# A new order for the opening of a gated-linear-attention and feed-forward kernel

## The chip, the cores and the metric

The kernel runs on one core of a Trainium2 chip. The metric is the device time of one execution in microseconds (us). A core has TensorE (PE in the profile; its weight loads are a row of their own, PEld), VectorE (DVE), ScalarE (ACT), GpSimd (POOL) and SyncE (SP). Each engine works through its own list of instructions in order and waits at an instruction until the semaphores that it names are reached. SP issues the DMAs here.

## The reference

Attention with a decaying state, per batch and head, and then a feed-forward layer with a squared ReLU:

```python
for t in range(S):
    state = alpha[:, :, t, :, None] * state + np.einsum('bhd,bhe->bhde', k[:, :, t], v[:, :, t])
    y[:, :, t] = np.einsum('bhd,bhde->bhe', q[:, :, t], state)
# x: y as (B*S, H*D)
h = np.maximum(x @ w_in, 0.0)
return (h * h @ w_out).astype(np.float32)
```

There are 4 batches, 8 heads, 768 positions and a head dimension of 48; x is 3072 x 384, w_in 384 x 2048 and w_out 2048 x 384. All is float32.

## The kernel before

The sequence is cut into blocks of 128 positions of one batch, with all eight heads: 24 blocks. Block n is chunk n // 4 of batch n % 4. Four blocks make a group of 512 rows of x, on which the feed-forward layer works: 16 products of 128 hidden columns (layer in), then the products with w_out (layer out). While TensorE works on the feed-forward layer of one group, the attention steps of the next blocks are woven in at planned times. Only the first four blocks (0 to 3) have nothing to be woven into. Their steps, together with the first loads, the first weight conversions and the first products of layer in, stand in a list of words written out by hand, `AT["first"]`; a loop near the end of the kernel runs the words in order, and each engine gets its instructions in that order. This list is the opening.

Before the list come the fixed preparations. POOL clears the state tiles s, the eight pads of the q and k tiles (16 unused columns beside each head's 48) and further tiles, and builds the identity and the triangle of ones (causal, rounded into causal_r; halves_mask is cut from it). VectorE clears two tiles am. `AT["pre"]` names the first loads, and three matmuls on a cleared tile (warm) follow.

The words of one block n, in the order of their data, with the lines of the kernel before:

- load: alpha (a), q, k, v of the block, one DMA each (L109). Some blocks use lent tiles (a_lent, qk_lent).
- ln (L261, ScalarE): logarithm of alpha. cs (L283, TensorE): its prefix sums, a product with the triangle, two passes of 384 columns. eb and ei (L294, L298, ScalarE): exponentials of the sums and of their negatives, called b and inv.
- mq, mk (L302, VectorE): q times b and k times inv, in place. qT, kT (L354, TensorE): turned by products with the identity, 128 x 512 in PSUM. qc, kc (L368): copied into SBUF as qs and ks.
- sc (L413, TensorE): the scores, 32 small products into two PSUM banks. kv (L442, TensorE): the sums of k times v into the same banks. am (L424, VectorE): the masked scores copied out. us (L456, VectorE): the first half's sum plus the old state. lt (L337 on TensorE, copied on ScalarE at L344): the last row of b turned. st (L477, L479, VectorE): the next state.
- For the pairs (0, 1) and (2, 3): ya and yb (L393, TensorE): the outputs y in two PSUM tiles, in two passes with a handshake through POOL between them. ep (L616): x rows copied out of y, 12 copies a pair, in four parts ep0 to ep3. The copies of the even and odd heads overlap in some rows, so that one waits for the other.

Weights come as raw halves of words: weights (L109) loads the next piece, first (L179, ScalarE) and second (L192 to L199, VectorE) convert it. Piece i serves products 2i and 2i + 1. ha and hb (L919) are a product of layer in on the first pair's rows and on the second pair's; ScalarE applies relu (L925) and square (L928). zeros n (L381) is n matmuls on a cleared tile, whose result nobody reads; so is warm (L237).

A copy of qc and kc goes to VectorE where the block's name stands in `AT["cp"]`:

```python
copy = nc.vector.tensor_copy if f"{x}{n}" in AT["cp"] else nc.scalar.copy
```

In the kernel before the names there end in a or b (q2a, k0b), so none matches and ScalarE makes all eight. `AT["evd"]` names the x copies of ep, as (block, even or odd heads, part), that VectorE makes; the others are ScalarE's.

Loads are paced by `move` (L109): an issue on SP waits for the earlier DMA that lies at least 2.25 us back by the costs given to each, 1.1 for a block's tensor and 2.3 for a piece of weights. Among tensors alone this is the fourth-last; behind a piece of weights it is the one ahead of the piece. So an issue marks the landing of an earlier load.

Of the kernel before, what the change touches and what calls it, by code (L numbers as in the profile page):

```python
# [9 lines left out]
FP32 = mybir.dt.float32  # L10
FP32R = mybir.dt.float32r
# [7 lines left out]


GB = 4
AT = {'thrp': 4.5, 'cvo': 3.35, 'thr': 2.25, 'm48': 16, 'cvs': 3.9, 'cv1': 0.125, 'later': (0, 0, 4, 6, 0, 1, 0), 'evs': 0.1, 'lead': 4, 'post': 3, 'w_first': (46.0, 38.0, 49.0), 'wstep': 1.0, 'w_in_at': 2.5, 'w_in_by': 3.6, 'room1': 22, 'room': 24, 's0': 4, 'ahead': 6, 'late': 2, 'xs': 0.0, 'g0': ((0.5, 4, False, True, 27.75), (25.75, 6, True, True), (29.25, 8, True, False)), 'sc0': (3.25, 2.35, 2.35), 'g1': ((5.5, 8, False, 15.0), (13.0, 10, True), (35.25, 12, True)), 'g': ((2.075, 6, True), (14.25, 8, True)), 'g1x': 51.0, 'gx': 48.75, 'g0x': 56.25, 'k0': 2, 'h0': 15, 'k1': 4, 'h1': 3, 'h1by': 2, 'evs0': 0.7, 'tp': 'ADMD', 'tp1': 'ADAD', 'split': 8, 'o0': (46.5, 48.5), 'o1': (), 'o2': (21.25, 24.75, 24.5, 40.0, 35.25, 28.25), 'str1': 21.5, 'ga': 9.75, 'gb': 12.5, 'cv0': -1.25, 'pre': '1a 0a 0q 0k 1k 1q', 'cp': ('q2a', 'k2b', 'k0a', 'k3a', 'k3b', 'k0b', 'q0b', 'q3b', 'q2b', 'q3a'), 'evd': ((0, 0, 0), (0, 0, 1), (0, 1, 2), (0, 1, 3), (2, 0, 3), (2, 1, 1), (2, 1, 2)), 'first': 'ln0 load1v cs0 ei0 eb0 zeros4 mk0 mq0 qT0 kT0 ln1 cs1 kc0 ei1 warm0 load0v eb1 mk1 qc0 weights0 lt1 sc0 load2a mq1 load2q kT1 kc1 qT1 load2k load3a qc1 load3k kv0 am0 first0 load3v sc1 ln2 kv1 load3q us0 am1 weights6 us1 cs2 ya0 ei2 second0 eb2 lt0 ln3 yb0 load2v mq2 qT2 mk2 load4a ep00 ep01 qc2 kT2 cs3 kc2 eb3 ei3 zeros1 sc2 ep02 mq3 mk3 kT3 ep03 weights2 first1 st0 ha0 second1 lt2 kv2 am2 qT3 load4k kc3 qc3 ha1 weights5 first2 sc3 kv3 am3 load4q us2 ha2 us3 ya2 yb2 weights3 ep20 ep21 ep22 load4v ep23 second2 first3 weights1 st1 weights4 ha3 lt3 hb0 st2 second3 hb2 hb3 hb1 st3'}


RUN = {0: 128, 32: 32, 64: 64, 96: 32}
# [3 lines left out]
def kernel(  # L29
# [12 lines left out]
    nc = tc.nc  # L42
    B, H, S, D = q.shape
    C = 128
# [19 lines left out]
    def kept(name, n, shape):  # L64
        return [consts.tile(shape, FP32, name=f"{name}{i}") for i in range(n)]

    s_all = kept("s", B + 2, [128, NP, 64])
    u_all = kept("us", 3, [128, NP, 64])
    for t in s_all[0:B]:
        nc.gpsimd.memset(t, 0.0)  # L70
    s_t = [s_all.pop(0) for _ in range(B)]
    NV = 4
    tiles = {
        "a": kept("a_in", 2, [128, H * D]), "q": kept("q_in", 2, [128, H, 64]),
        "k": kept("k_in", 3, [128, H, 64]), "v": kept("v_in", NV, [128, H * D]),
    }
    for t in tiles["q"] + tiles["k"]:
        nc.gpsimd.memset(t[:, :, D:64], 0.0)

    NW = 8  # L80
    wt_pool = ctx.enter_context(tc.tile_pool(name="wt", bufs=26))
# [2 lines left out]
    def two_k(name, dt=FP32, shape=(GB * C,)):  # L84
        return two_pool.tile([128, *shape], dt, tag="two", name=name)
# [40 lines left out]
    def need(*keys):  # L126
        for key in keys:
            assert key in given, key

    def load(n, xs="aqkv"):  # L130
        c, b = divmod(n, B)
        for x in xs:
            t = tile_of(x, n)
            if id(t) in owner:
                need(("free", *owner[id(t)]))
            owner[id(t)] = x, n
            given.add((x, n))
# [62 lines left out]

    for word in AT["pre"].split():
        load(int(word[0]), word[1:])
# [12 lines left out]
    ident = consts.tile([128, 128], FP32, name="ident")  # L215
    make_identity(nc, ident)
    causal = cv_pool.tile([128, C], FP32, tag="upper", name="causal")
    make_upper_triangular(nc, causal, 1.0, diag=True)
    causal_r = consts.tile([128, C], FP32R, name="causal_r")
    nc.gpsimd.tensor_copy(out=causal_r, in_=causal)  # L220
    halves_mask = consts.tile([128, C // 2], FP32, name="halves_mask")
    for i in range(2):
        rows = slice(64 * i, 64 * (i + 1))
        nc.gpsimd.tensor_copy(out=halves_mask[rows], in_=causal[rows, rows])
    for t in s_all + u_all:
        nc.gpsimd.memset(t, 0.0)
    last = consts.tile([128, 4, NP], FP32, name="last")
    nc.gpsimd.memset(last, 0.0)
# [7 lines left out]
    def warm(_):  # L236
        nc.tensor.matmul(  # L237
            out=ps_att.tile([128, NP, 64], FP32, tag="att", name="warm"),
            lhsT=s_t[0].rearrange("a p d -> a (p d)")[:, 0:128], rhs=s_t[0], start=True, stop=True,
        )  # L240

    for _ in range(3):
        warm(0)
# [11 lines left out]
    def work(name, bufs=1):  # L255
        return p2.tile([128, NP, C], FP32, tag=name, name=name, bufs=bufs)
# [7 lines left out]

    SPLIT = AT["split"]

# [162 lines left out]
    def am_h(n):  # L429
        t = am_t[n // 2 % NAM].rearrange("a e p t -> a (e p t)")  # L430
        return t.rearrange("a (e m p t) -> a e m p t", e=2, m=2, p=NP)

    def state_sums(n):
        need(("v", n), ("kb", n))
        given.add(("free", "k", n))
        ps = two[n]
        m = D if n >= AT["m48"] else 64
        for p in range(NP):
            for e in range(2):
                first = (2 * p + e) * D  # L440
                for h in range(1 if n // B == NCH - 1 else 2):
                    nc.tensor.matmul(  # L442
                        out=ps[h][64 * e : 64 * e + m, 1, p, G:64],
                        lhsT=tile_of("k", n)[HALF[h], 2 * p + e, 0:m],
                        rhs=tiles["v"][n % NV][HALF[h], first : first + D],
                        start=True, stop=True, skip_group_check=True,
# [17 lines left out]
    def rows_of(n):  # L464
        return [slice(0, D), slice(64, 64 + D)] if n >= AT["m48"] else [slice(0, 128)]

# [174 lines left out]
    here, todo, room = {}, [], [22]  # L641
# [92 lines left out]
    def in_x(j):  # L734
        acc["h", j] = ps_ffn.tile([128, GB * C], FP32, tag="att", name="h")
        in_passes(j, "b", "a", True, False)
        in_passes(j, "l", "l", False, True)
        x = acc["h", j]
        if kinds[0][j % 4] == "D":
            hid[j] = two_k("hid")  # L740
            nc.scalar.activation(out=hid[j], in_=x, func=AF.Copy, scale=E)  # L741
        else:
            nc.scalar.activation(out=x, in_=x, func=AF.Copy, scale=1.0 + E)  # L743

    def in_y(j):
        given.add(("hy", j))
        in_passes(j, "d", "d", False, True)
        if kinds[0][j % 4] == "D":
            combine(((hid[j], acc.pop(("h", j)), ALU.add, hid[j]),))

    kinds = [""]

    def in_post(j):
        need(("hy", j))
        given.add(("h", j))
        if kinds[0][j % 4] == "D":
# [7 lines left out]
        if kinds[0][j % 4] == "M":  # L764
# [212 lines left out]
    first = AT["first"]  # L977
# [129 lines left out]
    cv0 = AT["cv0"]  # L1107
    cvs = AT["cvs"]
# [70 lines left out]
```

## Time and profile before

| What | Value |
|---|---|
| Median of three runs | 518.93 us (517.73 to 519.45) |
| Profiled execution: span from first to last instruction | 518.6 us |
| Profiled execution: its own time beside the span | not listed; 0.3 us lie between the span and the median of the runs |
| TensorE busy | 507.8 us (98%) |
| VectorE, ScalarE, POOL busy | 355.7, 306.4, 5.3 us |
| TensorE busy from 0.00 to 5.67 us | 2.93 us, all of it on cleared tiles |
| TensorE busy from 15 to 25 us | 7.54 of 10 us |
| VectorE and ScalarE busy from 15 to 25 us | 9.50 and 7.77 of 10 us |
| TensorE busy from 25 to 37 us | 11.70 of 12 us |
| DMA engines' busy share from 15 to 37 us | 0.92 to 0.94 |

Times within the profile count from the first instruction. A row of a timeline gives start, length, engine, line, operation, output and inputs, and in brackets how long the engine had been idle and which instruction released it; x4 means four instructions drawn together. Lengths of neighbouring instructions overlap by about 0.1 us on VectorE and ScalarE, and by more on TensorE, so a chain is added up from start to start.

### The profile page before, as it was taken

How to read it: one execution, taken by the hardware profiler on the slowest of the kernel's cores; microseconds unless marked ns; L12 is line 12 of the kernel's file. 1: busy time of each engine (PE TensorE's matmuls, PEld its weight loads, DVE VectorE, ACT ScalarE, POOL GpSimd, SP SyncE). 2: the span in 40 equal slices, each digit the busy share in tenths (PEclk: the TensorE clock that was granted, in tenths of full speed). 3: DMA queues.
4: the chain of work that ended last, by engine and by line, in shares of the span. 5: the costliest groups of instructions: out<-in, count | busy, mean ns of one | idle time of the engine just before them, and what ended most of it. 6: DMA issues, size and time to landing. Idle time of an engine off the chain costs nothing.

```text
span 518.6 us, 13019 instructions
## 1 busy us (share of the span) xinstructions
PE 507.8 (98%) x5338; PEld 418.9 (81%) x5338; DVE 355.7 (69%) x628; ACT 306.4 (59%) x649; POOL 5.3 (1%) x29
## 2 busy tenths in 40 slices
PE   7899999999999999999999999999999999999997
PEld 5675455678888669987899988899988899988997
DVE  2766669986887877776697468587465487363861
ACT  4788898547888653485664276772275673164620
POOL 4000000000000000000000000000000000000000
PEclk9999999999999999999999999999999999999999
DMA  9999779472777786898884688864683545699201
GB/s 183 204 267 237 197 189 235 93 228 80 238 190 184 246 243 162 265 279 227 205 225 143 222 247 222 223 200 152 213 274 124 185 121 154 207 380 322 65 2 61
DMA packets 139323, 102.34 MB, mean 197 GB/s; under 512 B 109808, under 2 KB 115968, under 8 KB 139264
## 3 DMA queue, kind: packets, MB, share of 16 engines
q1 hardware_dynamic: 139264, 101.51, 68.2%
q8 instruction: 42, 0.69, 0.6%
q14 instruction: 17, 0.14, 0.1%
HBM read 84.16 MB, written 17.33 MB: 196 GB/s over the span
## 4 chain that ended last, share of the span: by engine, by line
PE 93%; DVE 4%; issue 1%; POOL 1%; ACT 1%; DVEq 0%; POOLq 0%
PE o L809 39%; PE h L726 32%; PE h L919 8%; PE y L393 4%; PE sckv L413 2%; PE T L578 2%; PE sckv L442 2%; PE cs L283 1%; PE cs L286 1%; DVE x L616 1%; PE cs L287 1%; DVE hd L648 1%; DVE hx L653 0%; DVE am L424 0%; ACT x L616 0%
## 5 line engine op out<-in xcount | busy, mean ns | idle before, releaser
L726 PE MATMUL h<-xd,wd 128*128 128x512 f32 x240 | 68.1, 396 | 1.1 <-issue 1.1
L726 PE MATMUL h<-xa,wb 128*128 128x512 f32 x240 | 68.7, 394 | 0.0
L726 PE MATMUL h<-xl,wl 128*128 128x512 f32 x240 | 67.9, 391 | 0.0
L648 DVE TENSOR_TENSOR hid<-h,hid 128x512 f32<-128x512 f32 x40 | 27.6, 689 | 51.1 <-PE h L726 51.0
L616 ACT COPY x<-y 48x256 f32<-48x256 f32 (+3 forms) x133 | 46.7, 365 | 21.2 <-PE y L393 18.8
L809 PE MATMUL o<-wb,ha 128*128 128x384 f32 x160 | 54.5, 340 | 0.0
L743 ACT ACTIVATE h<-h 128x512 f32<-128x512 f32 x40 | 23.3, 582 | 52.3 <-PE h L726 52.3
L809 PE MATMUL o<-wl,hl 128*128 128x384 f32 x160 | 53.7, 336 | 0.1
L809 PE MATMUL o<-wd,hd 128*128 128x384 f32 x304 | 53.7, 334 | 0.0
L809 PE MATMUL o<-w_out,hid 128*128 128x384 f32 x160 | 53.6, 489 | 0.0
L726 PEld LDWEIGHTS h<-xl,wl 128*128 128x128 f32 x240 | 45.1, 188 | 10.1 <-DVE xl L653 0.4
L809 PEld LDWEIGHTS o<-wd,hd 128*128 128x128 f32 x304 | 52.8, 188 | 0.0
L726 PEld LDWEIGHTS h<-xa,wb 128*128 128x128 f32 x240 | 44.4, 188 | 9.8 <-ACT hid L763 0.4
L726 PEld LDWEIGHTS h<-xd,wd 128*128 128x128 f32 x240 | 44.0, 188 | 9.1
L809 PE MATMUL o<-wb,hx 128*128 128x384 f32 x144 | 48.3, 336 | 0.0
L809 PE MATMUL o<-wl,hx 128*128 128x384 f32 x144 | 48.1, 334 | 0.0
L809 PEld LDWEIGHTS o<-w_out,hid 128*128 128x128 f32 x160 | 30.0, 190 | 19.7
L741 ACT ACTIVATE hid<-h 128x512 f32<-128x512 f32 x40 | 24.2, 606 | 32.9 <-PE h L726 32.5
L919 PE MATMUL h<-x,w_in 128*128 128x512 f32 (+1 forms) x120 | 43.4, 512 | 0.2 <-DVE x L616 0.2
L701 ACT ACTIVATE ha<-hid 128x512 fp32r<-128x512 f32 x40 | 25.1, 642 | 20.3 <-PE o L809 7.9
L919 PEld LDWEIGHTS h<-x,w_in 128*128 128x128 f32 x120 | 22.1, 190 | 17.8 <-issue 15.3
L653 DVE SCALAR_TENSOR_TENSOR hl<-ha,hid 128x512 fp32r<-128x512 f32 x40 | 27.5, 687 | 6.9 <-ACT ha L701 6.8
(111 smaller groups left out, 852.5 us busy)
## 6 DMA issues: line engine op xcount, KB each, us to landing
wd<-do SPq DMA_DIRECT2D x36, 384.0 KB
wl<-lo SPq DMA_DIRECT2D x34, 384.0 KB
wl<-li SPq DMA_DIRECT2D x32, 384.0 KB
wd<-di SPq DMA_DIRECT2D x32, 384.0 KB
raw<-in_moe_w_out_dram SPq DMA_DIRECT2D x8, 767.5 KB
raw<-in_moe_w_in_dram SPq DMA_DIRECT2D x8, 767.2 KB
v_in<-in_v_dram SPq DMA_DIRECT2D x24, 192.0 KB
out_dram<-osb SPq DMA_DIRECT2D x24, 192.0 KB
```

The costliest lines, as they stand in the source:

```text
L393: ins = nc.tensor.matmul(out=ys[e][64 * half : 64 * half + D + G * e, m % 2, p // 2, t], lhsT=lhsT, rhs=rhs, start=(half, e) not in seen, ...
L413: nc.tensor.matmul(out=ps[e][HALF[h], 0, p, :], lhsT=ks[rows, p, HALF[h]], rhs=qs[rows, p, HALF[h]], start=True, stop=True, skip_group_che ...
L442: nc.tensor.matmul(out=ps[h][64 * e : 64 * e + m, 1, p, G:64], lhsT=tile_of("k", n)[HALF[h], 2 * p + e, 0:m], rhs=tiles["v"][n % NV][HALF[ ...
L616: copy(out=x[kk][to : to + m, t : t + 2], in_=blk[n]["y"][e][r : r + m, :, p // 2],)
L648: nc.vector.tensor_tensor(out=o, in0=x, in1=z, op=op)
L653: nc.vector.scalar_tensor_tensor(out=o, in0=x, scalar=c, in1=y, op0=ALU.mult, op1=op)
L701: nc.scalar.activation(out=a, in_=x, func=AF.Copy, scale=NEAR * E)
L726: nc.tensor.matmul(out=acc["h", j], lhsT=here[w, "i", p][:, kk, jj * 128 : (jj + 1) * 128], rhs=x_parts[x][:, kk], start=start and kk == 0 ...
L741: nc.scalar.activation(out=hid[j], in_=x, func=AF.Copy, scale=E)
L743: nc.scalar.activation(out=x, in_=x, func=AF.Copy, scale=1.0 + E)
L809: nc.tensor.matmul(out=acc[t][:, 0:DM], lhsT=lhs[:, t * C : (t + 1) * C], rhs=rhs, start=start, stop=stop, skip_group_check=True,)
L919: nc.tensor.matmul(out=ps, lhsT=w[:, kk, c0 : c0 + 128], rhs=xT[g][kk][:, cols], start=(kk == 0), stop=(kk == KM - 1),)
```

## The change

Only the preparations and the opening's tables change.

- On POOL one state tile (s3) is cleared first, then the triangle, its rounded copy and the identity are made, and then the other clears follow. warm reads s3 instead of s0. The eight pads are cleared by VectorE, ahead of its two am tiles.
- `pre` loads k of block 1 ahead of k of block 0.
- `cp` becomes k0, k1, k2, q0, q1: these five turned tiles are copied by VectorE; q2, k3 and q3 stay with ScalarE.
- `evd`: for both pairs VectorE makes the copies of one of the two y tiles (six), ScalarE those of the other (six). Before, it was six and six in the first pair, five and seven in the second.
- `first` is a new list. ln1 and cs1 follow ln0 and cs0 directly; the first weights are loaded ahead of v1; zeros stand in five places (four of one matmul, one of four) where before there were zeros4 and zeros1; st0 stands ahead of the last x copies of the first pair; qT3 ahead of kT3; lt3 ahead of kv2; k3, v2 and v3 are loaded behind the second weights; hb1 is the first product on the second pair; ha4 and hb4 are added, so product 4 is made in halves here instead of whole behind the opening. first0 stands ahead of ln2 in both.
- `j % 4` becomes `j % len(kinds[0])`; the strings have four letters.

```diff
-'pre': '1a 0a 0q 0k 1k 1q', 'cp': ('q2a', 'k2b', 'k0a', 'k3a', 'k3b', 'k0b', 'q0b', 'q3b', 'q2b', 'q3a'), 'evd': ((0, 0, 0), (0, 0, 1), (0, 1, 2), (0, 1, 3), (2, 0, 3), (2, 1, 1), (2, 1, 2)), 'first': 'ln0 load1v cs0 ei0 eb0 zeros4 mk0 mq0 qT0 kT0 ln1 cs1 kc0 ei1 warm0 load0v eb1 mk1 qc0 weights0 lt1 sc0 load2a mq1 load2q kT1 kc1 qT1 load2k load3a qc1 load3k kv0 am0 first0 load3v sc1 ln2 kv1 load3q us0 am1 weights6 us1 cs2 ya0 ei2 second0 eb2 lt0 ln3 yb0 load2v mq2 qT2 mk2 load4a ep00 ep01 qc2 kT2 cs3 kc2 eb3 ei3 zeros1 sc2 ep02 mq3 mk3 kT3 ep03 weights2 first1 st0 ha0 second1 lt2 kv2 am2 qT3 load4k kc3 qc3 ha1 weights5 first2 sc3 kv3 am3 load4q us2 ha2 us3 ya2 yb2 weights3 ep20 ep21 ep22 load4v ep23 second2 first3 weights1 st1 weights4 ha3 lt3 hb0 st2 second3 hb2 hb3 hb1 st3'
+'pre': '1a 0a 0q 1k 0k 1q', 'cp': ('k0', 'k1', 'k2', 'q0', 'q1'), 'evd': ((0, 0, 0), (0, 0, 1), (0, 0, 2), (0, 0, 3), (2, 0, 0), (2, 0, 1), (2, 0, 2), (2, 0, 3)), 'first': 'ln0 ln1 load0v weights1 cs0 load1v cs1 eb0 mq0 ei0 warm0 qT0 zeros1 mk0 qc0 zeros1 kT0 load2a eb1 zeros4 ei1 mk1 kc0 zeros1 kT1 sc0 mq1 kc1 qT1 load2q load2k zeros1 qc1 kv0 am0 first0 load3a load3q lt1 sc1 kv1 ln2 lt0 us0 cs2 am1 eb2 us1 second0 ei2 ya0 weights6 load3k mq2 ln3 mk2 yb0 load2v load3v ep00 cs3 eb3 qT2 ep01 kT2 mq3 weights5 qc2 weights3 kc2 ei3 st0 ep02 qT3 sc2 ep03 mk3 am2 first1 ha0 kT3 weights4 kc3 qc3 ha1 lt3 first2 kv2 sc3 load4k second1 us2 kv3 am3 ha2 us3 ya2 lt2 yb2 st1 load4v ep20 ep21 ep22 ep23 weights0 st3 ha3 load4a hb1 first3 second2 load4q second3 hb0 st2 hb2 hb3 hb4 ha4 weights2'
...
-    for t in s_all[0:B]:
-        nc.gpsimd.memset(t, 0.0)
     s_t = [s_all.pop(0) for _ in range(B)]
+    nc.gpsimd.memset(s_t[3], 0.0)
+    causal = cv_pool.tile([128, C], FP32, tag="upper", name="causal")
+    make_upper_triangular(nc, causal, 1.0, diag=True)
+    causal_r = consts.tile([128, C], FP32R, name="causal_r")
+    nc.gpsimd.tensor_copy(out=causal_r, in_=causal)
+    ident = consts.tile([128, 128], FP32, name="ident")
+    make_identity(nc, ident)
...
-    for t in tiles["q"] + tiles["k"]:
-        nc.gpsimd.memset(t[:, :, D:64], 0.0)
+    pads = tiles["q"] + tiles["k"]
...
-        nc.gpsimd.memset(t[:, :, D:64], 0.0)
+        pads.append(t)
...
+    for t in pads:
+        nc.vector.memset(t[:, :, D:64], 0.0)
...
-    for t in s_all + u_all:
+    for t in s_t[0:3] + u_all + s_all:
         nc.gpsimd.memset(t, 0.0)
...
-            lhsT=s_t[0].rearrange("a p d -> a (p d)")[:, 0:128], rhs=s_t[0], start=True, stop=True,
+            lhsT=s_t[3].rearrange("a p d -> a (p d)")[:, 0:128], rhs=s_t[3], start=True, stop=True,
```

In the words weights0 to weights6 the figure has no effect: each loads the next piece, so both lists load pieces 0 to 6 in order.

More of the change, by code (lines that the diff above doesn't have):

```diff
@@ new lines @@
+AT = {'thrp': 4.5, 'cvo': 3.35, 'thr': 2.25, 'm48': 16, 'cvs': 3.9, 'cv1': 0.125, 'later': (0, 0, 4, 6, 0, 1, 0), 'evs': 0.1, 'lead': 4, 'post': 3, 'w_first': (46.0, 38.0, 49.0), 'wstep': 1.0, 'w_in_at': 2.5, 'w_in_by': 3.6, 'room1': 22, 'room': 24, 's0': 4, 'ahead': 6, 'late': 2, 'xs': 0.0, 'g0': ((0.5, 4, False, True, 27.75), (25.75, 6, True, True), (29.25, 8, True, False)), 'sc0': (3.25, 2.35, 2.35), 'g1': ((5.5, 8, False, 15.0), (13.0, 10, True), (35.25, 12, True)), 'g': ((2.075, 6, True), (14.25, 8, True)), 'g1x': 51.0, 'gx': 48.75, 'g0x': 56.25, 'k0': 2, 'h0': 15, 'k1': 4, 'h1': 3, 'h1by': 2, 'evs0': 0.7, 'tp': 'ADMD', 'tp1': 'ADAD', 'split': 8, 'o0': (46.5, 48.5), 'o1': (), 'o2': (21.25, 24.75, 24.5, 40.0, 35.25, 28.25), 'str1': 21.5, 'ga': 9.75, 'gb': 12.5, 'cv0': -1.25, 'pre': '1a 0a 0q 1k 0k 1q', 'cp': ('k0', 'k1', 'k2', 'q0', 'q1'), 'evd': ((0, 0, 0), (0, 0, 1), (0, 0, 2), (0, 0, 3), (2, 0, 0), (2, 0, 1), (2, 0, 2), (2, 0, 3)), 'first': 'ln0 ln1 load0v weights1 cs0 load1v cs1 eb0 mq0 ei0 warm0 qT0 zeros1 mk0 qc0 zeros1 kT0 load2a eb1 zeros4 ei1 mk1 kc0 zeros1 kT1 sc0 mq1 kc1 qT1 load2q load2k zeros1 qc1 kv0 am0 first0 load3a load3q lt1 sc1 kv1 ln2 lt0 us0 cs2 am1 eb2 us1 second0 ei2 ya0 weights6 load3k mq2 ln3 mk2 yb0 load2v load3v ep00 cs3 eb3 qT2 ep01 kT2 mq3 weights5 qc2 weights3 kc2 ei3 st0 ep02 qT3 sc2 ep03 mk3 am2 first1 ha0 kT3 weights4 kc3 qc3 ha1 lt3 first2 kv2 sc3 load4k second1 us2 kv3 am3 ha2 us3 ya2 lt2 yb2 st1 load4v ep20 ep21 ep22 ep23 weights0 st3 ha3 load4a hb1 first3 second2 load4q second3 hb0 st2 hb2 hb3 hb4 ha4 weights2'}
@@ L214 @@
     nc.scalar.preload_act_table_set("natural_log_exp_and_others")
[L215 to L220, printed above, removed]
     halves_mask = consts.tile([128, C // 2], FP32, name="halves_mask")
@@ L738, in in_x @@
         x = acc["h", j]
-        if kinds[0][j % 4] == "D":
+        if kinds[0][j % len(kinds[0])] == "D":
             hid[j] = two_k("hid")
@@ L747, in in_y @@
         in_passes(j, "d", "d", False, True)
-        if kinds[0][j % 4] == "D":
+        if kinds[0][j % len(kinds[0])] == "D":
             combine(((hid[j], acc.pop(("h", j)), ALU.add, hid[j]),))
@@ L755, in in_post @@
         given.add(("h", j))
-        if kinds[0][j % 4] == "D":
+        if kinds[0][j % len(kinds[0])] == "D":
             h = hid[j]
@@ L763, in in_post @@
         nc.scalar.activation(out=h, in_=acc.pop(("h", j)), func=AF.Relu)
-        if kinds[0][j % 4] == "M":
+        if kinds[0][j % len(kinds[0])] == "M":
             combine(((h, h, ALU.mult, h),))
```

1 line of the change is left out of this document (removed).

## The prediction, made before the changed kernel ran

> **What bounds the kernel now.** I read the page's busy shares first, then its 40 slices, then the opening instruction by instruction: TensorE's timeline, VectorE's, ScalarE's, and the DMA issues on SP.
>
> ```profile
> PE 507.8 (98%) x5338; PEld 418.9 (81%) x5338; DVE 355.7 (69%) x628; ACT 306.4 (59%) x649; POOL 5.3 (1%) x29
> ...
> PE   7899999999999999999999999999999999999997
> ```
>
> TensorE is the bound of nearly the whole span; only the first two slices (26 us) are short of nine tenths. The change rearranges just this stretch, so the most it can win is what TensorE loses there.
>
> ```profile
> 1.10 2.93 PE L237 MATMUL warm<-s 128*128 128x256 f32 x6 [1.10 <-POOL s L70]
> 5.67 1.62 PE L283 MATMUL cs<-a_in,causal_r 128*128 128x384 f32 x2 [1.64 <-POOL us L226]
> 7.08 1.92 PE L381 MATMUL zeros<-s 128*128 128x128 f32 x8
> 8.93 1.11 PE L354 MATMUL qT<-ident,q_in 128*128 128x128 f32 x4
> 10.35 0.81 PE L283 MATMUL cs<-a_in,causal_r 128*128 128x384 f32 x2
> ...
> 17.25 0.91 PE L283 MATMUL cs<-a_lent,causal_r 128*128 128x384 f32 x2 [1.06 <-ACT a_lent L261]
> ...
> 24.35 0.63 PE L354 MATMUL kT<-ident,qk_lent 128*128 128x128 f32 x4 [0.86 <-DVE qk_lent L302]
> 24.82 1.46 PE L919 MATMUL h<-x,w_in 128*128 128x256 f32 x6
> ...
> 35.60 1.23 PE L919 MATMUL h<-x,w_in 128*128 128x256 f32 x4
> 37.04 9.73 PE L919 MATMUL h<-x,w_in 128*128 128x256 f32 x32 [0.21 <-DVE x L616]
> ```
>
> The columns are start, length, instruction and, in brackets, idle time and its releaser. Useful work starts at 5.67 and is unbroken from 37.04 on. Between lie waits (1.06, 0.86), fillers (zeros, warm) and a slow stretch: prefix sums (cs) took 1.62 at 5.67 and 0.81 at 10.35. I compare both kernels at one point, the end of the first half product of the second pair of blocks (hb0 before, hb1 after): 37.04 + 0.43 = 37.47 before. All before it is equal work in both kernels; behind it TensorE has no wait for 200 us.
>
> ```profile
> 16.24 0.78 DVE L424 COPY_PREDICATED am<-halves_mask,sckv 128x256 f32<-128x256 uint32 x2 [0.19 <-PE sckv L442]
> ...
> 19.15 0.96 DVE L199 TENSOR_TENSOR w_in<-w_in,power 128x768 f32<-128x768 f32 x1
> 20.03 0.55 DVE L302 TENSOR_TENSOR qk_lent<-qk_lent,b 128x384 f32<-128x384 f32 x1
> ...
> 21.05 2.22 DVE L616 COPY x<-y 48x256 f32<-48x256 f32 x5
> ...
> 24.24 0.42 DVE L616 COPY x<-y 64x256 f32<-64x256 f32 x1
> ```
>
> From 16.24 to 24.66 VectorE never rests, and its last x copy releases ha0 at 24.82. That chain of 8.42 us, not TensorE, sets the middle of the opening.
>
> ```profile
> 5.04 0.52 ACT L261 ACTIVATE a_in<-a_in 128x384 f32<-128x384 f32 x1 [3.03 <-DMA a_in<-in_alpha_dram]
> ...
> 14.88 1.91 ACT L179 ACTIVATE power<-raw,rebias 128x768 uint16<-128x768 int16 x2
> 16.67 0.53 ACT L261 ACTIVATE a_lent<-a_lent 128x384 f32<-128x384 f32 x1
> ...
> 30.25 1.89 ACT L179 ACTIVATE power<-raw,rebias 128x768 uint16<-128x768 int16 x2
> ```
>
> Here the reader sees three DMA-bound starts: the first logarithm as alpha 0 lands, the conversion of weights 0 at 14.88, that of weights 2 at 30.25.
>
> **The triangle ahead of the clears.** The first cs (5.67) follows the logarithm that ends at 5.04 + 0.52 = 5.56. The triangle's cast was at 4.00 + 0.29 on POOL, 1.3 us ahead; making it sooner gains 0. The bracket's "POOL us" is a clear that happened to end then. The eight pad clears go to VectorE: the 1024-wide clear takes 0.91, a POOL pad clear 0.20, so 8 x 0.1 to 0.9 = 0.8 to 7.2; nearest in width is POOL's row, so about 1.6, ending near 4.7. VectorE's first real work is at 7.84, so 0; only the upper end would make it wait. POOL's remaining clears (it was done at 6.19) serve steps from 14.5 on: 0.
>
> **Prefix sums, fillers, first turns.** cs1 follows cs0 directly (7.08 to 8.36 slow) in place of the 1.71 us of zeros, then warm0 (slow, 0.85) to 9.21, then qT0, ready since 8.45. cs1, which ran at 10.35 to 11.0, is thus done early, but qT0 is 0.28 later. k0 is now loaded behind k1. SP's fourth-last rule makes the weight load wait for the fifth load: issued at 8.56, so k0 lands about 8.55, its product ends at 9.15, ahead of kT0 (10.5 after two one-matmul zeros). zeros4 and another (1.1 us) follow, so kT1 starts near 12.0 (13.22 before).
>
> **Copies on two engines.** No row shows VectorE copying 128x512 out of PSUM. On ScalarE it is 0.585. Bounds: VectorE's 256-wide x copy, 0.42, and two of them, 0.84; nearest is its 512-wide sum from PSUM (hid, 0.689), so 0.69, and 0.60 start to start, as its other rows overlap by 0.1. Queue on VectorE: qc0 10.25, mk1, kc0 to 12.0, mq1, kc1 (12.7, waits for kT1), qc1 13.8 to 14.5, am0 at 14.55 (15.04 before). Behind: lt1 0.46, sc1 0.52, kv1 0.58, and am1 at 16.1 (16.24 before). With 0.42 or 0.84 a copy, am1 moves by some 0.3 either way.
>
> **Loads.** Weights 0 go ahead of v1, which lands 0.6 to 1.1 us sooner, near 14.0 (14.66 before, where a3's issue waited for it). So its conversion ends near 16.0, ln2 at 16.7 and cs2 runs from 16.75: 0.5 earlier. But VectorE converts only behind us1 (16.9), so this early cs2 is cover, not gain. k3, v2 and v3 move behind weights 1; they are needed at 25.4, 28.5 and 29.4 and, at the 0.6 to 1.4 us between their landings and 3.1 for weights, are due by about 25. On SP the later issues wait only for DMAs and for buffers released by conversions.
>
> **VectorE's chain.** From am1 to the last x copy it gains kc2 (0.60) and the state step st0 (0.82, from 24.69 to 25.51 behind ha0's copies before) and loses mk3 (0.47): 8.42 + 0.95 = 9.37, so from 16.1 it ends at 25.47, 0.8 later than before. While it runs TensorE waits, mostly for mq3 (21.3 to 22.6). But qT3 and two thirds of ha0 run beneath its end, so only the last third of ha0 (0.43) follows: ha0 ends at 25.95, 0.26 sooner than before (24.82 + 1.39 = 26.21).
>
> **From ha0 to the second pair.** Before, 26.21 to 33.65 is 7.44. After: 0.46 more for lt3, 0.13 until mk3, 0.1 less as lt2 covers the POOL handshake between the two passes of y (32.95 to 33.02): 7.93, ending at 33.88. Then x: ScalarE starts 0.12 later, VectorE 0.39 behind it (a pair of copies overlaps in rows, 33.77 to 34.16), with six copies at 0.45 (six and six, where it was seven and five; the first pair had six and six already): 3.2, then 0.43 for the last third: 37.5. Before, this took 33.65 to 37.47 with lt3 (0.46) in it.
>
> Sum: 37.5 against 37.47, equal. With am1 at 15.8 and unhindered x copies (0.43, no handover) it is 0.7 earlier. I take the middle, 0.3 earlier. ha4 and hb4 replace one whole product, 6 x 0.43 either way: 0. `% len(kinds[0])` is 4 as before: 0. The profiled span is 518.6; only the span is given for that execution, 0.3 under the 518.93 median. Span 518.6 - 0.3, plus 0.3 to the median: 518.6.
>
> [...] The 128-column passes took 0.21 through 9.8 and 0.11 from 10.0, though the granted clock is 1.00 throughout; TensorE had then been busy 4.3 us. I keep the switch near 9.9: both kernels are busy from 5.67 without a gap. [...]
>
> **Rivals.** (a) *Slow clock for longer.* If cs1, warm0 and the turns do not wake the array by 10 and it stays slow till the scores, then qT0's rest, kT0, kT1, sc0 (some 1.5 us) double; VectorE's copies follow, and am1 comes 1.5 later: 520.1. For it: qT ran slow to 9.8. Against: before, the same mixture woke it. 0.06.
>
> (b) *Slower: ScalarE stuck at weights 2.* Its conversion first2 stands in order before ha2's relu, lt2's copies and the x copies at 34.0: 1.9 + 0.8 + 0.33, so weights 2 must land by 30.9; each us later costs one. They landed at 30.2 before, and the conversion waited for them (30.25). After, alpha 4 is no longer ahead (-0.7), but the issue waits for weights 1. From 33 on this decides for slower: 518.6 + 2.1 = 520.7 or more. With dearer copies (0.84, six on the path: +0.9) it takes less. 0.18.
>
> (c) *Faster: TensorE fed throughout.* If VectorE's chain did not hold ha0 (copies at 0.42, x copies well overlapped), TensorE goes from cs3 (19.85) through qT2, kT2, qT3, sc2, ha0 at 0.5, 0.5, 0.5, 0.6, 1.4 to 23.9 with its waits for mq2: 2 us sooner, 516.5. For it: the order offers work ahead of ha0. Against: 9.4 us of VectorE's rows cannot shrink by 2. A share of it (1.6) is enough. 0.22.
>
> **How the numbers follow.** A measurement here tells about 0.3% (1.6 us) from no change. Equal: 0.54, and rival (a), 0.06, falls inside that bound: same 0.60. Faster 0.22 from (c), slower 0.18 from (b). The range reaches into both: 516.7 (near (c)'s end) to 520.5 (near (b)'s).
>
> **What would show it.** cs0 still at 5.6 to 5.7; cs1 directly behind; the first VectorE copy of qT near 10.3 and 0.6 to 0.7 long; am1 near 16; VectorE without rest to 25.5; a TensorE wait of about 1.3 for mq3; ha0's last third near 25.5; weights 2's conversion by 30; TensorE unbroken from about 37. Wrong if ScalarE waits long for weights 2, if a bank wait appears that the rows cannot show, or if TensorE has waits behind 37.

## The result, and the profile after

The changed kernel took 524.14 us (median of 4 runs, 523.48 to 524.69) against 519.11 us for the kernel before on the same chip (4 runs, 517.73 to 519.45): a ratio of 1.0102, 95% interval 1.0086 to 1.0117. The forecast was no change, 518.6 us with a range up to 520.5. It was wrong: the kernel is 1.0% slower.

The page of the changed kernel, its busy shares, two rows of its 40 slices and one of its DMA queues (packets, MB, share of 16 engines):

```profile
PE 510.2 (98%) x5350; PEld 421.5 (81%) x5350; DVE 360.5 (69%) x642; ACT 304.5 (58%) x645; POOL 4.2 (1%) x21
PE   8899999999999999998999999999999999999997
PEclk9999999999999999998999999999999999999999
q8 instruction: 42, 0.69, 0.5%
```

TensorE has 12 matmuls and 12 weight loads more than before. Of the first two slices, which the change is about, the first is a little fuller (8 tenths in place of 7). New is a dent in the 19th slice (235 to 248 us), in TensorE's busy share and in its granted clock: 200 us behind the opening. The last line will matter below: 42 packets of 0.69 / 42 = 0.0164 MB, so 16 KB each, bring instructions.

First the opening. TensorE's timeline of the changed kernel (start, length, instruction, idle time and releaser):

```profile
5.41 2.90 PE L283 MATMUL cs<-a_in,causal_r 128*128 128x384 f32 x4 [1.39 <-ACT a_in L261]
...
8.67 0.60 PE L354 MATMUL qT<-ident,q_in 128*128 128x128 f32 x4
...
15.67 0.91 PE L283 MATMUL cs<-a_lent,causal_r 128*128 128x384 f32 x2
...
21.88 0.66 PE L354 MATMUL qT<-ident,qk_lent 128*128 128x128 f32 x4 [1.00 <-DVE qk_lent L302]
...
24.68 0.70 PE L919 MATMUL h<-x,w_in 128*128 128x256 f32 x2 [0.21 <-DVE x L616]
...
36.07 4.15 PE L919 MATMUL h<-x,w_in 128*128 128x256 f32 x18 [0.21 <-DVE x L616]
```

VectorE's timeline, and ScalarE's:

```profile
9.30 0.69 DVE L368 COPY qs<-qT 128x512 f32<-128x512 f32 x1 [0.27 <-PE qT L354]
...
13.86 0.78 DVE L424 COPY_PREDICATED am<-halves_mask,sckv 128x256 f32<-128x256 uint32 x2 [0.21 <-PE sckv L442]
...
15.33 0.78 DVE L424 COPY_PREDICATED am<-halves_mask,sckv 128x256 f32<-128x256 uint32 x2 [0.46 <-PE sckv L442]
...
23.30 1.33 DVE L616 COPY x<-y 48x256 f32<-48x256 f32 x3
```

```profile
12.29 1.88 ACT L183 ACTIVATE power<-raw,rebias 128x768 uint16<-128x768 int16 x2 [3.07 <-DMA raw<-in_moe_w_in_dram]
...
29.28 1.89 ACT L183 ACTIVATE power<-raw,rebias 128x768 uint16<-128x768 int16 x2 [0.97 <-DMA raw<-in_moe_w_in_dram]
```

The point of comparison, the end of the first half product of the second pair, is at 36.07 + 0.43 = 36.50, against 37.47 before: 0.97 us sooner. At the end of the opening this kernel is ahead. Most of that is not the change's doing, though: by the trace's record of the granted clock TensorE came to full speed at 8.36 us here and at 9.98 in the profiled execution before. A kernel that differs from before only by six tiny products (below) got its full clock at 8.52 and reached the first turns of block 4 at 65.30; the changed kernel got there at 65.07, and the kernel before, with its late clock, at 66.02. At equal clock some 0.2 us are left for the new opening.

The loss lies at 237 us. TensorE's timeline of the changed kernel there:

```profile
231.68 0.69 PE L413 MATMUL sckv<-qs,ks 48*64 48x64 f32 x32
232.19 0.63 PE L442 MATMUL sckv<-v_in,k_in 64*64 64x48 f32 x32
232.65 0.66 PE L393 MATMUL y<-qs,s 48*48 48x64 f32 x32
233.10 0.66 PE L393 MATMUL y<-qs,us 48*48 48x64 f32 x31
...
233.56 0.68 PE L393 MATMUL y<-am,v_in 64*48 64x64 f32 x30
237.09 0.36 PE L393 MATMUL y<-am,v_in 64*64 64x64 f32 x1 [2.85 <-issue]
237.38 1.65 PE L726 MATMUL h<-xd,wd 128*128 128x512 f32 x3
238.83 1.48 PE L726 MATMUL h<-xa,wb 128*128 128x512 f32 x3
...
240.97 0.86 PE L726 MATMUL h<-xd,wd 128*128 128x512 f32 x3
```

and of the kernel before at the same work:

```profile
234.56 0.68 PE L393 MATMUL y<-am,v_in 64*48 64x64 f32 x31
235.18 0.97 PE L726 MATMUL h<-xd,wd 128*128 128x512 f32 x3
...
239.08 0.40 PE L726 MATMUL h<-xd,wd 128*128 128x512 f32 x1 [1.11 <-issue]
```

Within one run of y products, all from the same tiles, TensorE stops for 2.85 us before one of them, and the releaser is "issue": nothing in the profile holds it. Then three products of 512 columns take 1.65 and 1.48 us in place of 0.86; the clock record says 0.5 from 237.05 for 3.41 us. Before, there was a stop of 1.11 us nearby, and no half clock. Lost here: 2.85 of waiting, 3.41 / 2 = 1.7 at half clock, and another "issue" wait of 0.53 at 340.5; less the 1.11 of before this is 4.0, less 0.95 of head start 3.0, close to the difference of the two profiled spans, 521.7 - 518.6 = 3.1. The medians differ by 5.0. The profiled execution of before was a long one of its kind: every later run lists its span, 1.8 us below its time, so a median of 519.11 belongs to a span of 517.3, and the changed kernel's 524.14 to one of 522.3. These two profiles don't locate the last 1 us. If a usual execution of before lacks the stop of 1.11, as one profile below does, the sum comes to about 5; this is not shown.

### The profile page after: what moved, and what is told of

Same layout as the page of the kernel before. It is cut to its first block, busy times and chain, and to the rows that moved or that the text cites. A ratio compares the mean times of both kernels' runs of the same rounds, so it can differ in the third digit from the quotient of the medians.

```text
span 521.7 us, 13045 instructions
## 1 busy us (share of the span) xinstructions
PE 510.2 (98%) x5350; PEld 421.5 (81%) x5350; DVE 360.5 (69%) x642; ACT 304.5 (58%) x645; POOL 4.2 (1%) x21
## 4 chain that ended last, share of the span: by engine, by line
PE 92%; DVE 5%; issue 1%; DMA 1%; ACT 0%; SPq 0%; DVEq 0%
PE o L809 39%; PE h L726 32%; PE h L919 8%; PE y L393 4%; PE sckv L413 2%; PE T L578 2%; PE sckv L442 2%; PE cs L283 1%; DVE x L616 1%; DMA a_in<-in_alpha_dram 1%; PE cs L286 1%; PE cs L287 1%; DVE hd L648 1%; DVE hx L653 0%; DVE am L424 0%
## 5 line engine op out<-in xcount | busy, mean ns | idle before, releaser
L616 ACT COPY x<-y 32x256 f32<-32x256 f32 (+1 forms) x132 | 46.4, 365 | 18.9 <-PE y L393 16.9
L183 ACT ACTIVATE power<-raw,rebias 128x768 uint16<-128x768 int16 x32 | 30.1, 992 | 5.4 <-DMA raw<-in_moe_w_in_dram 4.9
```

Of the source, the lines that this page charges most:

```text
L183: nc.scalar.activation(out=power[:, m], in_=top, func=AF.Relu, scale=8.0 * sign, bias=rebias)
L616: copy(out=x[kk][to : to + m, t : t + 2], in_=blk[n]["y"][e][r : r + m, :, p // 2],)
```

## The experiments

**The suspicion.** TensorE's instructions (matmuls, weight loads and the few for semaphores), counted through the trace, have every long "issue" wait at a place of the same remainder by 256: number 5570 in the changed kernel, 5569 in the kernel before (one less; that its trace lacks a record is my guess), and 8130 = 5570 + 10 x 256. The instruction queue moves 16 KB packets, so 64 bytes an instruction if a packet is 256 of them. For the packets the trace gives start and end:

```
block that begins with number 5570   TensorE enters    packet of         first instr. of
                                     the one ahead     this block        this block
after                                232.15            233.89 - 235.66   237.09
before                               233.33            236.80 - 237.73   239.08
```

In these two places the packet of the block starts 1.7 and 3.5 us after TensorE has entered the block ahead of it, takes 1.8 and 0.9 us, and the block's first instruction runs 1.4 us behind its end. Elsewhere that is hidden: of the 84 block boundaries in the two profiles 81 have no "issue" wait of TensorE, and the third that has one is the 0.53 us at 340.5. 256 instructions of large products last longer (two packets near the end of the changed kernel, at 450.68 and 478.55 us, lie 28 us apart). But the 256 that end at 234.24 in the changed kernel are scores, state sums and y alone, used up in 2.1 us. My theory: the change adds 24 TensorE instructions ahead of this place (12 matmuls and their weight loads), so the boundaries fall 24 instructions earlier in the work behind it, and one falls so that a block holds nothing but tiny products. The rival: the work itself, the new opening, costs.

**24 instructions into the kernel before.** Six products of one column on a cleared tile (four instructions each) behind the first warms, where TensorE idles:

```diff
     for _ in range(3):
         warm(0)
+    pad_to = padded[-1]
+    for i in range(6):
+        e, p = i % 2, i // 2 % NP
+        nc.tensor.matmul(
+            out=pad_to[64 * e : 64 * e + D, 0, p : p + 1], lhsT=s_t[0][:, 0, 0:D], rhs=s_t[0][:, 0, D : D + 1],
+            start=True, stop=True, skip_group_check=True,
+        )
```

(`padded` keeps warm's PSUM tiles.)

> The kernel before with 6 such one-column products behind the warms, 24 TensorE instructions more, so that the block boundary 5570 falls on the same work as in the changed kernel. Theory (instruction blocks): a wait of 2 to 3 us near 238 followed by half clock for 3.4 us, 521.5 to 523.5 us in place of 519.1, with nothing of the change in it. Rival (the new opening itself): no effect, 519.1.

Measured: 523.95 us (523.91 to 524.34), ratio 1.0094 (1.0078 to 1.0111). The whole loss, with nothing of the change. Its timeline shows the same stop and the same slow products:

```profile
237.47 0.26 PE L404 MATMUL y<-am,v_in 64*64 64x64 f32 x1 [2.99 <-issue]
237.67 1.65 PE L737 MATMUL h<-xd,wd 128*128 128x512 f32 x3
```

**24 instructions out of the kernel after.** Its zeros4 and two of its zeros1 are left out:

```diff
-... mk0 qc0 zeros1 kT0 load2a eb1 zeros4 ei1 ... load2k zeros1 qc1 ...
+... mk0 qc0 kT0 load2a eb1 ei1 ... load2k qc1 ...
```

> The changed kernel without zeros4 and two of the zeros1: 6 products of zeros, 24 TensorE instructions fewer. Theory (instruction blocks): the boundary falls where it fell in the kernel before, the wait at 237 shrinks to about 1.1 us and the clock stays up: 520 to 521.5. The fillers themselves stand in TensorE's waiting time; taking 1.3 us of them out moves the opening by -0.5 to 0.3. Rival (the new opening itself): 523.5 to 524.5.

Measured: 518.53 us (517.41 to 519.75), ratio 0.9988 (0.9975 to 1.0000): better than the 520 to 521.5 expected, and no longer slower. In its profile the boundary cost 0.24 us, in the middle of a run of large products, and no half clock follows:

```profile
236.01 0.62 PE L726 MATMUL h<-xd,wd 128*128 128x512 f32 x2 [0.24 <-issue]
```

**96 instructions into the kernel after.** The same products on its cleared tile:

```diff
+    for i in range(24):     # s_t[3] in place of s_t[0]
```

> The changed kernel with 24 one-column products of zeros into the last warm tile behind the three warms: 96 more TensorE instructions (24 products, each two weight loads and two passes) in a stretch where TensorE idles anyway. Theory (instruction blocks): TensorE's instructions come in blocks of 256 (16384 bytes); the wait of 2.85 us at 237 is the fetch of the block that begins at instruction 5570, because the block ahead of it lies wholly on scores, state sums and y and is used up in 2.1 us, while the fetch lands 3.5 us after that block is entered. 96 instructions more put the block's start some 6 us earlier, into the products of layer in, so it lasts over 7 us and hides the fetch: no wait near 237, no stretch of half clock, 519 to 520.5 us in place of 524.1. Rival (the new opening itself delays TensorE at 237, through its loads or buffers): the wait stays, 524.

Measured: 526.08 us (523.11 to 526.53), ratio 1.0122 (1.0089 to 1.0154). I missed the time. The stop at 237 is gone, but the boundaries found other places. TensorE's timeline and its list of waits (in total, times, longest):

```profile
23.36 0.33 PE L404 MATMUL y<-am,v_in 64*48 64x64 f32 x3 [2.64 <-issue]
23.62 1.65 PE L294 MATMUL cs<-a_lent,causal_r 128*128 128x384 f32 x2
```

```profile
PE y L404 <- issue: 4.5, 3, 2.6
...
PE sckv L453 <- issue: 0.9, 1, 0.9
PE o L820 <- issue: 0.9, 1, 0.9
```

The stop is now in the opening's y products, again with 3.41 us at half clock behind it, and smaller ones lie at 17.1, 121.4, 207.3 and 263.9. This shift cured one place and hurt five.

**The same 24 instructions ahead of the place and behind it.** This leaves the opening alone. In the kernel before the first six score products of one block are made a second time into the same place, in block 4 (75 us) or in block 21 (342 us):

```diff
+        for i in range(6 if n == 4 else 0):     # or n == 21
+            p, h, e = i // 4, i // 2 % 2, i % 2
+            rows = slice(64 * e, 64 * e + D)
+            nc.tensor.matmul(
+                out=ps[e][HALF[h], 0, p, :], lhsT=ks[rows, p, HALF[h]],
+                rhs=qs[rows, p, HALF[h]], start=True, stop=True, skip_group_check=True,
+            )
```

> The kernel before, with the first 6 score products of block 4 (near 75 us) made a second time into the same place: 24 more TensorE instructions, 0.26 us of products by the row of block 4's scores (0.69 us for 16), the opening untouched. Theory of blocks: the boundary near 237 us lies 24 instructions earlier in the work, as in the kernel after: a wait of 2.6 to 3.1 us there, 3.4 us at half clock, a second wait of 0.5 to 1.1 near 340: 522.5 to 524.5 us. Rival (the loss is made in the opening and only shows later): 519.2, no wait above 1.2.

> The same 24 instructions at block 21 (near 342 us), behind the boundaries at 237 and 340 us. Theory of blocks: all that lies ahead is as in the kernel before, and the boundary near 394 us has over 5 us to be fetched: 518.9 to 519.7 us, with the wait of about 1 us at 239 that the kernel before has. Rival (24 more instructions cost wherever they are): as block 4's, 522 us or more.

Measured: block 4, 524.37 us, ratio 1.0107 (1.0065 to 1.0149); block 21, 519.22 us, ratio 0.9997 (0.9985 to 1.0008). TensorE's timeline with block 4's:

```profile
238.64 0.26 PE L393 MATMUL y<-am,v_in 64*64 64x64 f32 x1 [3.26 <-issue]
238.84 1.65 PE L733 MATMUL h<-xd,wd 128*128 128x512 f32 x3
```

and with block 21's, where no wait appears at the place of before's stop of 1.11:

```profile
237.42 0.84 PE L733 MATMUL h<-xd,wd 128*128 128x512 f32 x3
238.19 0.69 PE L393 MATMUL y<-am,v_in 64*48 64x64 f32 x32
```

The same instructions cost 5 us ahead of the place and nothing behind it. This settles the cause: not the opening, not the work, not the number of instructions, but how many stand ahead of the blocks' dense place. In this profile even the kernel before's own wait of 1.1 was missing: the packet started 2.05 us after TensorE entered the block ahead, where before it was 3.47.

**A whole block, and parts of 24.** The same added products as in the first of these runs, 64 of them (256 instructions), 2 (8) and 4 (16):

```diff
-    for i in range(6):
+    for i in range(64):     # or 2, or 4
```

> The kernel before, with 64 one-column zero products (256 TensorE instructions, four per product) behind the opening's warms, where TensorE idles until 5.7 us. Theory of blocks (TensorE gets its instructions in blocks of 256, and a block whose predecessor is used up in about 2 us comes late): a shift by a whole block leaves every later boundary at the same instruction, so the time stays within 0.3% of the kernel before, 518.3 to 520.3 us, with its wait of about 1 us near 239 us and no stretch at half clock there. Rival (any instruction added ahead costs, by its number): ten times as many as the 24 that cost 4.9 us, so far over 524 us. Rival (it is the added work in the opening, not the alignment): 524 us or more, with the loss before 70 us.

Measured: 521.97 us (520.05 to 523.32), ratio 1.0047 (1.0028 to 1.0066): above what I gave the theory and below what I gave the rivals. No stop came, as expected: the longest "issue" wait is 0.2 us, where I had expected the 1 us of before, and the clock is full from 11 us on. What the profile shows of the loss is in the opening, where the filling was not free:

```profile
3.95 3.14 PE L251 MATMUL warm<-s 128*48 128x1 f32 x128
7.03 1.10 PE L294 MATMUL cs<-a_in,causal_r 128*128 128x384 f32 x2
```

64 products took 3.14 us and held the first prefix sum until 7.03, 1.4 us later than before. That is about half of the median's 2.55; the rest I can't name, as the profiled execution is one of the shortest (520.3). The record gives a sign: by the clock record this execution had full clock from 4.21, half clock from 7.62 to 11.04 and full clock again behind it. The five executions with such a stretch (a granted clock of 0.997) took 520.05 to 521.76 us, the five with 1.00 522.18 to 523.32. So the rest may lie in how the clock started; no profile shows it for the longer ones.

> The kernel before, with 2 one-column zero products (8 TensorE instructions). Theory of blocks: moved back by 8 instructions, the boundary near 237 us leaves about 3.6 us between the entry of one block and the first use of the next, where before had some 4.9 and 24 more instructions 2.1; at 5.0 to 5.2 us for request and fetch the wait is about 1.5 us in place of 1.1, and one of about 1.4 comes near 340 us. No stretch at half clock, since a wait of 1.56 us brought none in an earlier run: 519.5 to 521.5 us. If half clock follows already, 522 to 523. Rival (count alone): 4.9 us times 8/24, so 520.4, with no wait that grows.

Measured: 519.52 us, ratio 1.0009 (0.9988 to 1.0029), waits of 0.51 and none at 340: less than the 1.5 and 1.4 expected.

> The kernel before, with 4 one-column zero products (16 instructions) behind the warms. Theory of blocks: by the times of the kernel before, 3.0 us lie between entry and first use at 236 us and 3.3 at 338 (24 instructions: 2.2 and 2.3; 8: 3.9 and 3.8, which measured 0.5 and 0): waits of 1.5 to 2.3 at 237 and 0.3 to 1.2 at 340; 519.5 to 521.5 us without half clock, 522 to 524 with it. It tells whether the loss comes in steps or grows with the shift.

Measured: 520.76 us, ratio 1.0023 (1.0005 to 1.0042). At 238.9, at number 5570, the wait is 0.72 us, which the profile puts down to VectorE; I had said 1.5 to 2.3. There is no half clock at that place (this execution has one in its opening, from 18.39 to 25.22 us, behind a wait of 1.90 for alpha). Its first turns of block 4 came at 68.05, 2.0 us later than before, so the loss of this execution lies in the opening and not at the boundary. 8 instructions thus cost nothing that can be told, 16 some 0.2% that the profile doesn't show to be the blocks', 24 nearly 1%: the loss does not grow evenly with the number. My sizes failed because the packet's start is not fixed: it came 0.8 us (16 instructions), 1.6 (8), 1.7 (after), 2.1 (block 21), 2.7 (24), 2.95 (block 4) and 3.5 us (before) after TensorE entered the block ahead. What delays it was not tried.

**20 instructions out of the kernel before.** Its zeros4 and zeros1 are left out, which should move the boundary near 316 us into tiny products:

```diff
-... eb0 zeros4 mk0 ... ei3 zeros1 sc2 ...
+... eb0 mk0 ... ei3 sc2 ...
```

> The kernel before without its five zeros products (20 TensorE instructions less). Theory of blocks: the boundary near 316 us moves 20 instructions later in the work, where by the times of the kernel before only 2.0 us lie between the entry of one block and the first use of the next, and the one near 395 us has 3.0: waits of about 2.5 to 3 near 316 (with 3.4 us at half clock) and of 1 to 2 near 395, and the wait at 239 grows no longer than 1: 521.5 to 525 us, although work was taken away. Rival (fewer instructions are cheaper, by count): 518 or less; the opening alone, with TensorE idle for 1.9 us more while its clock is still slow: 518.5 to 520 with no wait at 316.

Measured: 520.36 us (520.02 to 522.43), ratio 1.0023 (1.0006 to 1.0041). My forecast of new stops missed: there is none at 316 or 395. The packet of that block started at 313.18, 0.5 us before TensorE entered the block ahead. That block, too, was used up in 1.9 us (313.68 to 315.61), and the next ran on without a stop. So a dense block alone did not make the stop; where it came, a late packet came with it (started 1.7 us after the entry in the changed kernel). Here large products stood ahead of the block; that this brought the packet earlier is my guess, and no run shows it. The slow part is the opening, as the second rival had it, a little above its 518.5 to 520. From TensorE's timeline:

```profile
8.90 1.12 PE L354 MATMUL qT<-ident,q_in 128*128 128x128 f32 x4 [1.64 <-DVE q_in L302]
9.81 1.06 PE L354 MATMUL kT<-ident,k_in 128*128 128x128 f32 x4
10.66 1.49 PE L283 MATMUL cs<-a_in,causal_r 128*128 128x384 f32 x2
```

Without the filler TensorE rested 1.64 us, its clock came to full speed at 12.34 us (9.98 before), and the first turns of block 4 were 1.0 us later.

**The new opening's parts.** All turned copies back on ScalarE, in the kernel after:

```diff
-'cp': ('k0', 'k1', 'k2', 'q0', 'q1')
+'cp': ()
```

> The changed kernel with all eight turned tiles copied by ScalarE (the list cp empty); as many TensorE instructions. Theory of the opening (VectorE's chain from am1 to the last x copy sets ha0): the chain loses kc2's 0.6 us, so the first turns of block 4 (65.1 in the changed kernel, 66.0 before) come at 64.5 to 65.2; the wait at 237 stays, 523 to 524.5. Rival (ScalarE is the bound of the opening, and the copies on VectorE are what gained 0.9): first turns of block 4 at 65.7 or later, 524.5 or more.

Measured: 522.79 us (518.92 to 523.82), ratio 1.0067 (1.0045 to 1.0090); in its profile, a short execution of 520.2 us, the stop at 236.15 was 1.56 us and no half clock followed. The first turns of block 4 came at 65.38, between what the theory and the rival said. The five executions with a granted clock of 0.996 or 0.997 took 522.73 to 523.82 us, the three with 0.999 or 1.00 518.92 to 521.50: this fits half clock behind the stop in those five, though no profile shows where in them it lay. The loss by the blocks covers what the copies do, so the two were tried at equal blocks, with the 24 instructions left out:

> The kernel after less 24 instructions of zeros (its blocks lie as before), and with all eight turned copies on ScalarE. If VectorE's queue of copies and masks sets the opening, as the prediction's sum has it, taking five copies of 0.69 us from VectorE ends its chain sooner, while ScalarE's weight conversions move later by as much; the sum leaves 0.5 us either way: 518.0 to 519.3 us against 518.5 with VectorE's copies. Rival (the two-engine copies are the gain of this change): over 520 us.

Measured: 518.20 us, ratio 0.9975 (0.9964 to 0.9986). Then both on one chip:

> Once more the kernel after less 24 instructions of zeros, beside the next kernel. Earlier it stood at 0.9988 of the kernel before. Theory: with the blocks back where they lay, the new opening is worth 0.2 to 0.7 us at equal clock and saves part of the 1 us wait at 239: 0.997 to 1.000. Rival (the opening itself gains nothing): 1.000 to 1.002.

> The same with all turned copies on ScalarE, earlier at 0.9975, on another chip than the kernel above. If the copies on VectorE are the change's worth, it is slower than the kernel above by 0.5 us or more; if they hold VectorE's chain, as the prediction had it, faster by 0.3 to 1 us; if neither engine's copies end last, within 0.3 us.

Measured: 518.15 us, ratio 0.9985 (0.9976 to 0.9993), with VectorE's copies, and 518.18, ratio 0.9985 (0.9975 to 0.9995), with ScalarE's. Which of the two engines makes the copies is worth nothing that can be told. The opening as a whole, without these six fillers and at the blocks of before, is worth 0.15%, 0.7 us: less than the 1.6 us that I called measurable, though these intervals leave 1 out. Part of it can be a smaller stop at the boundary (0.70 us in the profile of the first, none in the second's, 1.11 in before's). These two are the fastest kernels of the study, ahead of both given ones.

Only the preparations (triangle first, pads on VectorE, warm on s3, k of block 1 loaded first), with the kernel before's list; against the kernel before, in its core:

```diff
-    for t in s_all[0:B]:
-        nc.gpsimd.memset(t, 0.0)
     s_t = [s_all.pop(0) for _ in range(B)]
+    nc.gpsimd.memset(s_t[3], 0.0)
+    causal = cv_pool.tile([128, C], FP32, tag="upper", name="causal")
+    make_upper_triangular(nc, causal, 1.0, diag=True)
...
+    for t in pads:
+        nc.vector.memset(t[:, :, D:64], 0.0)
...
-'pre': '1a 0a 0q 0k 1k 1q'
+'pre': '1a 0a 0q 1k 0k 1q'
```

> The kernel before, with only the new order of the preparations: the triangle ahead of the clears, the pads cleared by VectorE, warm on s3, and k of block 1 loaded ahead of k of block 0; no TensorE instruction more or less. The prediction priced this at nothing, since the first prefix sum waits for the logarithm: 518.4 to 519.2 us, the first prefix sum at 5.4 to 5.7. Rival (the triangle was late): 0.3 us or more sooner in the opening. Theory of blocks: no new wait near 237 us.

Measured: 521.33 us, ratio 1.0032 (1.0017 to 1.0048), where I had priced all of it at nothing. VectorE's timeline, then TensorE's:

```profile
8.41 0.56 DVE L302 TENSOR_TENSOR k_in<-k_in,inv 128x384 f32<-128x384 f32 x1 [4.28 <-DMA k_in<-in_k_dram]
8.88 0.55 DVE L302 TENSOR_TENSOR q_in<-q_in,b 128x384 f32<-128x384 f32 x1
```

```profile
9.59 1.08 PE L354 MATMUL qT<-ident,q_in 128*128 128x128 f32 x4 [1.11 <-DVE q_in L302]
```

The old list has the product for k ahead of the one for q on VectorE. With k0 landing late both wait, then the turn of q, and the clock comes to full speed at 12.65. The new list has them the other way round, so this price does not arise there. With the old order of loads:

```diff
-'pre': '1a 0a 0q 1k 0k 1q'
+'pre': '1a 0a 0q 0k 1k 1q'
```

> The kernel before with the triangle made ahead of the clears, the pads on VectorE and warm on s3, but k of block 0 loaded ahead of k of block 1 as before. The earlier kernel with both took 1.0032 of the time before, and its VectorE waited 4.3 us for k of block 0, until 8.4 us, with q of block 0 behind it. If that order of loads was its loss: 0.999 to 1.001, the turn of q within 0.3 us of 8.9. If the pads on VectorE or the triangle were: 1.002 to 1.005 again.

Measured: 519.83 us, ratio 1.0012 (1.0002 to 1.0021), the turn of q at 8.58. The order of loads was thus most of that loss; the triangle and the pads bring no gain, and at most some 0.1% the other way, which lies outside what I expected by a hair and has no new wait in the opening. Its profile has "issue" waits of 0.56 us at 238.06 and, new, of 0.49 at 320.26; what moved them is open.

## Why the prediction was wrong

**The step that failed** is in the first part, "behind it TensorE has no wait for 200 us", used as if it held for both kernels, together with the prices of the added TensorE instructions: the fillers by their length in the opening, and "ha4 and hb4 replace one whole product, 6 x 0.43 either way: 0". I counted their time and not their number. The runs put 5 us in the place of that 0: 24 instructions ahead of 237 us cost about 5 us in a kernel with the old opening, in its idle time or in block 4 alike, and leaving 24 out gives the new opening 518.5. None of the three rivals was this one. The text did name "TensorE has waits behind 37" as what would make it wrong, without a mechanism, a place or a chance. The view was there: the wait of 1.11 us for "issue" at 239.08 stands in the list of waits of the kernel before, the longest behind the opening, and I did not ask what it was.

**The opening's sum was right.** It said equal to 0.7 sooner by the second pair, 0.3 taken; at equal clock the profiles give about 0.2, and the times with the blocks back in place 0.7 us. By its parts:

- Triangle: the first prefix sum at 5.41, released by the logarithm that ended at 5.3; gain 0, as said. Pads: VectorE was through at 4.14 (about 4.7 forecast), hidden.
- Copy of 128 x 512 on VectorE: 0.69 us, the value taken between 0.42 and 0.84.
- VectorE's chain from the second mask to the last x copy: 15.33 to 24.63, 9.30 us; forecast 9.37. Its beginning was 0.8 sooner than the 16.1 forecast; the early clock accounts for 0.5 of that, as the turn of q took 0.60 in place of 1.1.
- TensorE's wait for the product mq3: 1.00 at 21.88; forecast 1.3 between 21.3 and 22.6.
- Weights 0: landed by 12.29, not near 14.0, so cs2 ran at 15.67 and not 16.75. Mis-sized by 1.7 us, and, as said, cover and not gain.
- Weights 2: converted from 29.28, ahead of the 30.9 of rival (b). That rival did not come. Rival (c), 2 us sooner, did not come either: the chain held the last third of ha0 until 24.68, as the sum had it.
- Slow clock: "I keep the switch near 9.9" was wrong in kind. It came between 4.0 and 12.65 us in the profiles here, at 4.39 and 10.45 in the last two kernels with the 24 left out, which begin with the same TensorE instructions. The prediction read the granted clock as 1.00 throughout; the clock record of before begins at 9.98 and tells nothing of the time ahead of it. That busy time of TensorE brings the switch, as the prediction and its rival (a) took it, is not shown. In the clock records of before and of the changed kernel each stretch but the last is a multiple of 3.413 us long (508.59 = 149 x 3.413; 228.69 = 67 x, 3.41 and 279.89 = 82 x), and the two records begin at 9.98 and 8.36 us.

**The conversion to a time** was off too: the sum took the profiled span of before for a typical one, 0.3 us below the time. Spans lie 1.8 below the times, so that execution was 1.3 long. It cancels in the difference and didn't cause the miss.

## What to carry to other kernels

A stop of TensorE that the profile puts down to "issue" in a dense stretch of tiny matmuls is to be counted in instructions from the start: if all such stops have one remainder by 256, as numbers 5570 and 8130 had here, an edit that changes the number of TensorE instructions ahead can move them, and its price can appear far behind it. Here 24 instructions cost some 5 us at 237 to 239 us, some 230 us behind those in the opening and 160 behind those in block 4. Compare an opening's variants at an equal number of instructions (a few one-column products, or fillers left out, set it), or the alignment is measured in place of the edit. Ask of the longest unexplained wait of the profile before what it is, even where the change does not touch it.

## What the runs showed of the hardware

- TensorE's instructions come 256 at a time here (42 packets of 16 KB for 10,859 instructions of the changed kernel, and its "issue" waits at numbers 5570 and 8130). At 81 of 84 boundaries in the profiles of before and of the changed kernel no "issue" wait shows. The long stops were 2.85, 2.99 and 3.26 us in three kernels where a block was used up in 2.1 us, and 2.64 us in the opening with 96 more, where it was used up in 3.7 us and the next packet started only 3.9 us after its entry.
- Half clock came behind long waits of TensorE. Waits of 2.64, 2.85, 2.99 and 3.26 us were each followed by 3.41 us at half clock; waits of 1.11, 1.35 and 1.56 us in the long run of the kernel were not. No limit follows from this: in two openings half clock came among tiny products behind single waits of 1.90 us (16 instructions, from 18.39) and 0.63 us (24 left out, copies on ScalarE, from 17.28), and with the whole block added from 7.62, behind 3.14 us of one-column products and no wait.
- 64 one-column products of zeros took 3.14 us, 49 ns each, so that a shift by a whole block is not free.
